# Down projection with tokens stationary: 128 tokens of g held, 512 columns of w_out moving

## The chip, the cores and the metric

The kernel runs on one core of one Trainium2 chip. The metric is the device time of one execution in microseconds (us). Before the change it is 959.91 us, the median of three runs (959.44 to 959.99).

Engines are named as in the profile: PE (TensorE matmul) with PEld (its weight loads), DVE (VectorE), ACT (ScalarE), POOL (GpSimd), and SP, whose queue issues all DMAs here.

## The reference

Attention over 8 batches, 8 heads, 576 positions and 64 dimensions, in two parts that are added: a pooled one (q, k and v averaged over groups of four positions, softmax over 144 pooled keys, the result repeated four times) and a local one (softmax over keys less than four positions away). The heads are joined to 512 features per token, and the 4608 tokens go through two projections.

```python
out_d = sm_attn(q_d, k_d, v_d)               # pooled by 4
out_up = np.repeat(out_d, factor, axis=2)
mask = np.abs(pos[:, None] - pos[None, :]) < factor
out_local = softmax(where(mask, scale * q @ k.T, -1e9)) @ v
x = (out_up + out_local).transpose(0, 2, 1, 3).reshape(B * S, H * D)
h = x @ w_in                                  # 512 -> 2048
g = np.maximum(0.01 * h, h)
return g @ w_out                              # 2048 -> 512
```

## The kernel before, in words

**Tokens in chunks.** `plan` (L42) cuts the tokens into 13 chunks, the columns of one matmul. Batch 0 makes chunk 0 (256 tokens) and chunk 1 (320). Batches 1 to 7 have 9 blocks of 64 tokens each (a block is every ninth position), and `SIZES` deals the 63 blocks out: 4, 5 and then 6 to a chunk, so 256, 320 and nine times 384 columns. A chunk is made of segments of at most `MAXSEG` blocks of one batch; PARTS lists them by batch.

**Three matmuls for each product.** Weights, x and g are kept as a high part that the fast float32 matmul takes exactly and a low part that is the rest. A product is high by high, high by low and low by high.

**Up projection** (`up_proj`, L689). For each chunk and each f of 16 slices of 128 features of h, twelve matmuls (four slices of x, three products) fill a bank `hp` with 128 features by the chunk's tokens. `leaky` (L712) then makes the high part gh and the activation itself by ACT (L716, L717), and the low part gl by DVE (L719).

**Down projection** (`down_proj`, L724). For each f and each e of four slices of 128 output features, three matmuls (L746) hold 128 by 128 of w_out in the array and move gh or gl, the chunk's tokens being the columns; they add into bank `acc{e}`. The result is the output transposed (features by tokens). After the last f, `store` (L765) copies each bank to a buffer `o` (two of them) and writes it out.

**Passes.** Weights for f = 8 to 15 come late (their memory is given back by batch 0's attention, `swap`, L792). So PASSES runs chunk 0 and chunk 1 over f = 0 to 7, then both over f = 8 to 15, and then each later chunk over all 16. The half sums are stored to the output in memory, loaded again (`refetch`, L757) and added by DVE (L771).

**Making x.** Batch 0 goes through PE with banded scores (`banded`, L434); its two halves fill x of chunks 0 and 1. For later batches the local part is done per segment and pair of heads: `scores` (L548) and `values` (L602) let POOL multiply into `prod` (L567, L628) and DVE add up (L573, L634); `landing` (L658) transposes the result by PE (L665), adds the pooled part (L672) and writes the high part by ACT (L678) and the low part by DVE (L680). The pooled part (`pooled`, L330) is scores by PE (L358), softmax by ACT and DVE, transposes (L397) and values (L409). x has two pairs of buffers, for even and odd chunks; a chunk's x may be written once the chunk two before it is done.

**Weights.** `convert` (L255) loads 512 KB of a float64 weight slice into a staging buffer, builds float32 from its bits by ACT (L268) and DVE (L270), makes the high part by ACT (w_in, L281) or DVE (w_out, L278), and the low part by POOL (L283). Staging buffers are borrowed from k, v, prod and up for f below 10 and from v, up and vs after, with two x buffers besides for the first four.

**Order.** Nothing is ordered on the chip but by waits. `Order` (L98) runs all of this as tasks in a model with costs for each engine (COST, RATE, HOP) and a buffer count for each tag (`bufs`, L190); at each step it emits the operation that the model could start first, at equal times the one with the smallest rank. Up and down projection have the last ranks (4999, 5000). So each engine's queue is a fixed list, and a wrong cost in the model shows as a wait. Small matmuls use two banks `pt`; batch 0 may use the accumulators and `hp` until the up projection has started (`banks`, L291).

Of the kernel before, what the change touches and what calls it, by code (L numbers as in the profile page):

```python
# [27 lines left out]
MAXSEG = 4  # L28
SIZES = (4, 5, 6, 6, 6, 6, 6, 6, 6, 6, 6)
QB = 48  # L30
FSPLIT = 8
OWN = 10
# [40 lines left out]
LANDED = [NC, NC] + [2 * sum(len(pieces(a, z)) for _, a, z, _ in c[2]) for c in CHUNKS[2:]]  # L73
XMAX = [max(c[1] for c in CHUNKS[i::2]) for i in range(2)]
OMAX = max(XMAX)
# [11 lines left out]
class Slot:  # L87
    def __init__(self, order, tag, index, t, task):
        self.order, self.tag, self.index, self.t, self.task = order, tag, index, t, task
        self.push = HURRY if tag in SCARCE else 0  # L90
        task[0] -= self.push
# [91 lines left out]
def attn_moe(ctx: ExitStack, tc, qkt, vd, qb, kb, vb, vwb, band, identb, w_in, w_out, ident, edge, out):  # L183
# [6 lines left out]
    bufs = dict(head=HEADS, qk=1, vs=1, qk_d=2, v_d=1, su_vd=2, su_half=1, su_pd=3, su_ptd=2, st_d=3, pd=2, ptd=1, outd=2, q=1, k=1, v=1, s=3, st_l=3, prod=2, up=1,  # L190
                xloc=2, lst=3, gh=3, gl=3, o=2, hp=2, pt=2, xh0=1, xl0=1, xh1=1, xl1=1, acc0=1, acc1=1, acc2=1, acc3=1,
# [3 lines left out]
    def slot(*tags):  # L195
        return (yield ("slot", tags, 0))
# [24 lines left out]
    def wait(name, n=1):  # L221
        return (yield ("wait", name, n))
# [32 lines left out]
    def convert(f, k):  # L255
        s = yield from slot(*(("k", "v", "prod", "up") if f < OWN else ("v", "up", "vs")), *(("xh1", "xl1") if f < 4 else ()))
# [25 lines left out]
        t = yield from op("POOL", 590, t)  # L282
        nc.gpsimd.tensor_tensor(out=lo, in0=tf, in1=hi.bitcast(F32), op=ALU.subtract)  # L283
# [4 lines left out]
    xt = {}  # L288
    kept = {}
# [11 lines left out]
    def x_tile(i):  # L301
        if i > 1:
# [27 lines left out]
    def pooled(b, c, rank, pool=None):  # L330
# [20 lines left out]
        s_st, s_pd = (yield from slot("st_d")), (yield from slot("su_pd" if pool else "pd"))  # L351
# [10 lines left out]
        st, pd = sb(s_st, [128, 2, 3], F32), sb(s_pd, [128, 3, SD], F32, pool)  # L362
# [71 lines left out]
    def banded(b, c, hf, rank, pool=None):  # L434
# [90 lines left out]
        t = yield from op("ACT", n, t, tx)  # L525
        nc.scalar.copy(out=xh[:, c], in_=av[:, :n])
        t = yield from op("DVE", n, t)
        nc.vector.tensor_tensor(out=xl[:, c], in0=av[:, :n], in1=xh[:, c].bitcast(F32), op=ALU.subtract)
        s_b.free(t)
        od.signal(("x", hf), t)  # L530
# [71 lines left out]
    def values(i, b, j0, j1, c0, u):  # L602
# [4 lines left out]
        s_v = yield from slot("v")  # L607
# [79 lines left out]
    reload = {}  # L687
# [36 lines left out]
    def down_proj():  # L724
        for i, (p, f) in enumerate(steps):
            ch, f0, f1 = PASSES[p]
            n = CHUNKS[ch][1]
            per = 0.012 + n / 2400
            if f == f0:
                accs[p] = {}  # L730
            if f == f0 + 2 and f0 > 0:
                for e in range(NE):
                    od.spawn(50, refetch(p, e, n))
            tg = yield from wait(("g", i))
            tw = yield from wait(("w", f, 1))
            s_g, s_l, gh, gl = gs.pop(i)
            wh, wl = (w.rearrange("p c m -> p (c m)") for w in weight(f, 1))
            for e in range(NE):
                if f == f0:
                    s_a = yield from slot(f"acc{e}")  # L740
                    accs[p][e] = s_a, bank(s_a)
                s_a, acc = accs[p][e]
                es = slice(e * 128, (e + 1) * 128)
                t = yield from op("PE", 3 * per, tg, tw, s_a.t)
                for j, (wt, g) in enumerate(((wh, gh), (wh, gl), (wl, gh))):
                    nc.tensor.matmul(acc[:, :n], wt[:, es], g[:, :n],  # L746
                                     start=f == f0 and j == 0, stop=f == f1 - 1 and j == 2)
# [5 lines left out]
    def dest(p, e, n):  # L753
        base = CHUNKS[PASSES[p][0]][0]
        return out[e * 128:(e + 1) * 128, base:base + n]

    def refetch(p, e, n):  # L757
        s_o = yield from slot("o")
        o = sb(s_o, [128, OMAX], F32)
        tw = yield from wait(("half", PASSES[p][0]), 4)  # L760
        t = yield from load(o[:, :n], dest(p, e, n), 512 * n, s_o.t, tw)
        reload[p, e] = s_o, o
        od.signal(("reload", p, e), t)

    def store(p, e, n, s_a, acc, t):  # L765
        key, f0, f1 = PASSES[p]
        if f0 > 0:
            tr = yield from wait(("reload", p, e))
            s_o, o = reload.pop((p, e))
            t = yield from op("DVE", n, t, tr)  # L770
            nc.vector.tensor_tensor(out=o[:, :n], in0=acc[:, :n], in1=o[:, :n], op=ALU.add)  # L771
        else:
            s_o = yield from slot("o")
            o = sb(s_o, [128, OMAX], F32)
            if p == len(PASSES) - 1 and e % 2:
                t = yield from op("DVE", n, t, s_o.t)
                nc.vector.tensor_copy(out=o[:, :n], in_=acc[:, :n])
            else:
                t = yield from op("ACT", n, t, s_o.t)
                nc.scalar.copy(out=o[:, :n], in_=acc[:, :n])  # L780
        s_a.free(t)
        t = yield from load(dest(p, e, n), o[:, :n], 512 * n, t)
# [49 lines left out]
_OUTS = [((DM, B * S), 'float32')]  # L832
# [56 lines left out]
```

## Time and profile before

| | |
|---|---|
| time, median of three runs | 959.91 us |
| span of the profiled execution | 957.9 us |
| PE busy | 932.4 us, 97% |
| POOL busy | 617.8 us, 64% |
| DVE busy | 595.2 us, 62% |
| ACT busy | 415.0 us, 43% |
| mean granted clock of PE | 0.996 |

The span runs from the first to the last instruction of the program; the time of an execution is larger by what lies around it. A busy share is an average over the span. Matmuls are pipelined: a matmul's recorded length (some 0.34 us at 384 columns) overlaps those of its neighbours, so the price of one in a stream is the distance between starts. Line numbers (L746) are those of the kernel before. In the lists of waits a row reads: who waited, for whom, us in total, times, longest. In the groups: count, busy us, mean ns of one, idle time before them and what ended it.

### The profile page before, as it was taken

The numbers are of one execution on the slowest core, as the hardware profiler recorded it, in microseconds if no ns is written. First come the engines' busy times: TensorE is split into PE (matmuls) and PEld (weight loads), VectorE is DVE, ScalarE is ACT, GpSimd is POOL, SyncE is SP. The second block draws the span as 40 slices with busy tenths as digits, with TensorE's granted clock in tenths as the row PEclk, the third lists the DMA queues.
The fourth block names the chain that finished last, engine by engine and source line by source line (L and its number), as shares of the span: only waits on it lengthen the run. The fifth ranks groups of instructions, "written<-read, shape, count | busy, mean of one in ns | idle before, by whom it ended". The sixth has DMA issues, their size and how long they took to land.

```text
span 957.9 us, 16170 instructions
## 1 busy us (share of the span) xinstructions
PE 932.4 (97%) x6282; PEld 894.8 (93%) x6282; DVE 595.2 (62%) x895; ACT 415.0 (43%) x1139; POOL 617.8 (64%) x356
## 2 busy tenths in 40 slices
PE   6799999999999999999999999999999999999997
PEld 5588999899999999999999999899999999999997
DVE  5986678888887776787657774862753753311111
ACT  3774555555545543445324553532513423422211
POOL 3759868777888778986798776884885873100000
PEclk9899999999999999999999999999999999999999
DMA  9755665644554523452424442431231220000000
GB/s 264 241 184 181 214 201 179 189 164 145 188 166 122 190 96 116 131 187 95 135 74 146 159 148 101 140 116 58 92 116 58 91 77 31 34 1 1 34 1 33
DMA packets 63180, 117.31 MB, mean 122 GB/s; under 512 B 4944, under 2 KB 32848, under 8 KB 63104
## 3 DMA queue, kind: packets, MB, share of 16 engines
q1 hardware_dynamic: 63104, 116.29, 38.6%
q8 instruction: 49, 0.80, 0.4%
q14 instruction: 27, 0.22, 0.1%
HBM read 105.65 MB, written 10.62 MB: 121 GB/s over the span
## 4 chain that ended last, share of the span: by engine, by line
PE 77%; POOL 8%; DMA 4%; issue 4%; DVE 4%; ACT 2%; SPq 0%; POOLq 0%; DVEq 0%; ACTq 0%
PE hp L706 35%; PE acc L746 34%; POOL prod L567 4%; POOL prod L628 3%; PE pt L358 2%; DMA k<-in_kb_dram 2%; PE pt L397 2%; PE pt L409 2%; PE pt L665 1%; DMA qk<-in_qkt_dram 1%; DVE s L573 1%; DMA v<-in_w_in_dram 0%; SPq L218 0%; DMA vs<-in_w_out_dram 0%; DVE gl L719 0%
## 5 line engine op out<-in xcount | busy, mean ns | idle before, releaser
L567 POOL TENSOR_TENSOR prod<-q,k 128x1344 f32<-128x1344 f32 (+1 forms) x88 | 266.3, 3027 | 81.3 <-DMA k<-in_kb_dram 55.2
L628 POOL TENSOR_TENSOR prod<-v,s 128x1344 f32<-128x1344 f32 (+1 forms) x88 | 265.6, 3021 | 32.3 <-DVE xloc L634 18.2
L706 PE MATMUL hp<-xh,wih 128*128 128x384 f32 (+2 forms) x832 | 279.9, 336 | 5.8 <-DVE gl L719 5.1
L746 PE MATMUL acc<-gh,woh 128*128 128x384 f32 (+2 forms) x832 | 274.4, 330 | 0.3 <-ACT o L780 0.3
L706 PE MATMUL hp<-xl,wih 128*128 128x384 f32 (+2 forms) x832 | 269.5, 324 | 0.3 <-DVE xl L680 0.3
L706 PE MATMUL hp<-xh,wil 128*128 128x384 f32 (+2 forms) x832 | 269.6, 324 | 0.0
L746 PE MATMUL acc<-gh,wol 128*128 128x384 f32 (+2 forms) x832 | 269.0, 323 | 0.0
L746 PE MATMUL acc<-gl,woh 128*128 128x384 f32 (+2 forms) x832 | 268.9, 323 | 0.0
L719 DVE TENSOR_TENSOR gl<-hp,gh 128x384 fp32r<-128x384 f32 (+2 forms) x208 | 108.5, 522 | 215.7 <-ACT hp L717 215.2
L716 ACT ACTIVATE gh<-hp 128x384 fp32r<-128x384 f32 (+2 forms) x208 | 97.3, 468 | 315.6 <-PE acc L746 307.9
L706 PEld LDWEIGHTS hp<-xh,wih 128*128 128x128 f32 x832 | 156.4, 188 | 15.6 <-DVE gl L719 8.0
L746 PEld LDWEIGHTS acc<-gh,woh 128*128 128x128 f32 x832 | 156.2, 188 | 4.0 <-issue 3.2
L706 PEld LDWEIGHTS hp<-xl,wih 128*128 128x128 f32 x832 | 156.7, 188 | 0.5 <-DVE xl L680 0.5
L706 PEld LDWEIGHTS hp<-xh,wil 128*128 128x128 f32 x832 | 156.4, 188 | 0.0
L746 PEld LDWEIGHTS acc<-gl,woh 128*128 128x128 f32 x832 | 156.3, 188 | 0.0
L746 PEld LDWEIGHTS acc<-gh,wol 128*128 128x128 f32 x832 | 156.2, 188 | 0.0
L573 DVE TENSOR_REDUCE s<-prod 128x21 f32<-128x1344 f32 (+1 forms) x88 | 130.2, 1479 | 27.9 <-POOL prod L567 27.9
L634 DVE TENSOR_REDUCE xloc<-prod 128x192 f32<-128x1344 f32 (+1 forms) x88 | 130.1, 1478 | 22.5 <-POOL prod L628 22.1
L717 ACT ACTIVATE hp<-hp 128x384 f32<-128x384 f32 (+2 forms) x208 | 96.1, 462 | 0.0
L672 DVE TENSOR_TENSOR pt<-pt,up 128x384 f32<-128x384 f32 (+1 forms) x44 | 37.8, 861 | 27.6 <-PE pt L665 22.2
L652 ACT COPY up<-outd 128x576 f32<-128x576 f32 x84 | 52.3, 675 | 0.0
L370 ACT ACTIVATE pd<-pt,st_d 128x144 f32<-128x144 f32 x84 | 32.1, 382 | 46.4 <-DVE st_d L367 35.4
(154 smaller groups left out, 754.3 us busy)
## 6 DMA issues: line engine op xcount, KB each, us to landing
k<-in_kb_dram SPq DMA_DIRECT2D x38, 576.0 KB
v<-in_vb_dram SPq DMA_DIRECT2D x38, 576.0 KB
qk<-in_qkt_dram SPq DMA_DIRECT2D x32, 576.0 KB
vs<-in_vd_dram SPq DMA_DIRECT2D x28, 288.0 KB
q<-in_qb_dram SPq DMA_DIRECT2D x38, 192.0 KB
out_dram<-o SPq DMA_DIRECT2D x36, 192.0 KB
v<-in_w_out_dram SPq DMA_DIRECT2D x4, 512.0 KB
prod<-in_w_out_dram SPq DMA_DIRECT2D x4, 512.0 KB
```

The source lines that it names most:

```text
L370: nc.scalar.activation(out=pd[:, qi], in_=scv[:, qi], func=AF.Exp, scale=SCALE / (FAC * FAC), bias=mx[:, qi:qi + 1], accum_out=sm[:, qi:qi ...
L567: nc.gpsimd.tensor_tensor(out=prv, in0=q[:, p, a - j0:z - j0].unsqueeze(2).to_broadcast([128, n, W, D]), in1=view(k[:, p], (a - j0) * D, [ ...
L573: nc.vector.tensor_reduce(out=s[:, p, a - j0:z - j0], in_=prv, axis=AX.X, op=ALU.add)
L628: nc.gpsimd.tensor_tensor(out=prv, in0=view(v[:, p], a - j0, [[1, n], [nv, D], [1, W]]), in1=s[:, p, a - j0:z - j0].unsqueeze(2).to_broadc ...
L634: nc.vector.tensor_reduce(out=xl_t[:, :n, p], in_=prv, axis=AX.X, op=ALU.add)
L652: nc.scalar.copy(out=up[:, pp], in_=outd[b][:, 2 * u + pp].unsqueeze(2).to_broadcast([128, SD, FAC]))
L672: nc.vector.tensor_tensor(out=xv, in0=xv, in1=upv, op=ALU.add)
L706: nc.tensor.matmul(hp[:, :n], wt[:, c], x[:, c], start=k == 0, stop=k == 3 * NC - 1)
L716: nc.scalar.activation(out=gh[:, :n], in_=hp[:, :n], func=AF.Prelu, alpha=0.01)
L717: nc.scalar.activation(out=hp[:, :n], in_=hp[:, :n], func=AF.Prelu, alpha=0.01)
L719: nc.vector.tensor_tensor(out=gl[:, :n], in0=hp[:, :n], in1=gh[:, :n].bitcast(F32), op=ALU.subtract)
L746: nc.tensor.matmul(acc[:, :n], wt[:, es], g[:, :n], start=f == f0 and j == 0, stop=f == f1 - 1 and j == 2)
```

## The change

- **Down projection.** Now 128 tokens of gh or gl are held in the array and all 512 columns of a slice of w_out move. A chunk has two or three tiles of 128 tokens, each with a bank `acc{m}`, and the output is written as tokens by features.
- **First chunks kept in PSUM.** Chunk 0 uses banks 0 and 1, chunk 1 banks 2 and 3, and they stay until f = 15; storing, loading and adding half sums go. Once chunk 1 is stored, bank 3 is given to the small matmuls as a third bank besides the two `pt`.
- **Chunks.** All are multiples of 128 tokens: 256, 256, 256 and ten times 384. Batch 0's last 64 tokens ride at the end of chunk 2 (`TAIL`), behind three blocks of batch 1. Segments have at most three blocks.
- **Stores.** A tile leaves in two halves of 256 columns, each with its own copy and DMA (`send`), from three buffers `o`; in the last chunk DVE takes every second copy.
- **Buffers.** A new tag `w2` serves as a second v buffer and as staging for weights. su_pd goes from 3 to 2, pd from 2 to 1, s and st_l from 3 to 2.
- **Low parts.** For f from 8 on (`LOV`) the low part of a weight is made by DVE.

```diff
-MAXSEG = 4
-SIZES = (4, 5, 6, 6, 6, 6, 6, 6, 6, 6, 6)
+MAXSEG = 3
+SIZES = (3,) + (6,) * 10
+TT = 128
+OW = 256
-OWN = 10
+OWN, LOV = 10, 8
+STAGE = "w2", "up", "v"
-    chunks, at = [(0, 256, ()), (256, 320, ())], S
+    chunks, at = [(0, 256, ()), (256, 256, ())], 512
+        n += i == 0
+TAIL = (2, CHUNKS[2][1] - 64)
+X0 = 256 - TAIL[1]
...
     def convert(f, k):
-        s = yield from slot(*(("k", "v", "prod", "up") if f < OWN else ("v", "up", "vs")), *(("xh1", "xl1") if f < 4 else ()))
+        s = yield from slot(*(("k", "v", "w2", "prod", "up") if f < OWN else STAGE), *(("xh1", "xl1") if f < 4 else ()))
...
-        t = yield from op("POOL", 590, t)
-        nc.gpsimd.tensor_tensor(out=lo, in0=tf, in1=hi.bitcast(F32), op=ALU.subtract)
+        if f >= LOV:
+            t = yield from op("DVE", 512, t)
+            nc.vector.tensor_tensor(out=lo, in0=tf, in1=hi.bitcast(F32), op=ALU.subtract)
+        else:
+            t = yield from op("POOL", 590, t)
+            nc.gpsimd.tensor_tensor(out=lo, in0=tf, in1=hi.bitcast(F32), op=ALU.subtract)
...
     def banks(b):
+        if "spare" in od.events:
+            return "pt", "acc3"
...
     def values(i, b, j0, j1, c0, u):
-        s_v = yield from slot("v")
+        s_v = yield from slot("v", "w2")
...
     def down_proj():
+        per = 0.0133 + DM / 2400
         for i, (p, f) in enumerate(steps):
             ch, f0, f1 = PASSES[p]
-            n = CHUNKS[ch][1]
-            per = 0.012 + n / 2400
-            if f == f0:
-                accs[p] = {}
-            if f == f0 + 2 and f0 > 0:
-                for e in range(NE):
-                    od.spawn(50, refetch(p, e, n))
+            tiles = CHUNKS[ch][1] // TT
+            if f == 0:
+                accs[ch] = {}
...
-            for e in range(NE):
-                if f == f0:
-                    s_a = yield from slot(f"acc{e}")
-                    accs[p][e] = s_a, bank(s_a)
-                s_a, acc = accs[p][e]
-                es = slice(e * 128, (e + 1) * 128)
+            for m in range(tiles):
+                if f == 0:
+                    s_a = yield from slot(f"acc{m + 2 * (ch == 1)}")
+                    accs[ch][m] = s_a, bank(s_a)
+                s_a, acc = accs[ch][m]
+                ms = slice(m * TT, (m + 1) * TT)
                 t = yield from op("PE", 3 * per, tg, tw, s_a.t)
-                for j, (wt, g) in enumerate(((wh, gh), (wh, gl), (wl, gh))):
-                    nc.tensor.matmul(acc[:, :n], wt[:, es], g[:, :n],
-                                     start=f == f0 and j == 0, stop=f == f1 - 1 and j == 2)
-                if f == f1 - 1:
-                    od.spawn(-5, store(p, e, n, s_a, acc, t))
+                for j, (g, wt) in enumerate(((gh, wh), (gh, wl), (gl, wh))):
+                    nc.tensor.matmul(acc, g[:, ms], wt, start=f == 0 and j == 0, stop=f == NF - 1 and j == 2)
+                if f == NF - 1:
+                    od.spawn(-5, store(ch, m, s_a, acc, t))
...
+    def store(ch, m, s_a, acc, t0):
+        rows = CHUNKS[ch][0] + m * TT
+        ends = []
+        for h in range(DM // OW):
+            cols = slice(h * OW, (h + 1) * OW)
             s_o = yield from slot("o")
+            o = sb(s_o, [128, OW], F32)
+            if ch == len(CHUNKS) - 1 and h % 2:
+                t = yield from op("DVE", OW, t0, s_o.t)
+                nc.vector.tensor_copy(out=o, in_=acc[:, cols])
             else:
+                t = yield from op("ACT", OW, t0, s_o.t)
+                nc.scalar.copy(out=o, in_=acc[:, cols])
+            ends.append(t)
+            if h == DM // OW - 1:
+                s_a.free(max(ends))
+                if ch == 1 and m == 1:
+                    od.signal("spare", max(ends))
+            od.spawn(-4, send(out[rows:rows + TT, cols], o, s_o, t))
```

More of the change, by code (lines that the diff above doesn't have):

```diff
@@ L70, in pieces @@
     return list(zip(cuts, cuts[1:]))
-LANDED = [NC, NC] + [2 * sum(len(pieces(a, z)) for _, a, z, _ in c[2]) for c in CHUNKS[2:]]
-XMAX = [max(c[1] for c in CHUNKS[i::2]) for i in range(2)]
-OMAX = max(XMAX)
+TAIL = (2, CHUNKS[2][1] - 64)
+X0 = 256 - TAIL[1]
+LANDED = [NC, NC] + [(NC if c is CHUNKS[2] else 0) + 2 * sum(len(pieces(a, z)) for _, a, z, _ in c[2]) for c in CHUNKS[2:]]
+OMAX = max(c[1] for c in CHUNKS)
+assert all(c[1] % TT == 0 for c in CHUNKS)
 COST = {"ACT": (0.13, 0.00083), "DVE": (0.08, 0.00104), "POOL": (0.25, 0.00217)}
@@ L89, in __init__ @@
         self.order, self.tag, self.index, self.t, self.task = order, tag, index, t, task
[L90 removed]
+        self.push = HURRY if tag in SCARCE or (tag == "acc3" and "spare" in order.events) else 0
         task[0] -= self.push
@@ L301, in x_tile @@
     def x_tile(i):
-        if i > 1:
+        if i == 2:
+            t = yield from wait(("done", 0), 2)
+            xt[i] = [x[:, :, X0:X0 + CHUNKS[i][1]] for x in whole]
+            od.signal(("xbuf", i), t)
+            return
+        if i > 2:
             yield from wait(("xbuf", i - 1))
@@ L306, in x_tile @@
         s_h, s_l = (yield from slot(f"xh{i % 2}")), (yield from slot(f"xl{i % 2}"))
-        xt[i] = [sb(t, [128, NC, XMAX[i % 2]], F32R)[:, :, :CHUNKS[i][1]] for t in (s_h, s_l)]
+        full = [sb(t, [128, NC, OMAX], F32R) for t in (s_h, s_l)]
+        if i == 0:
+            whole.extend(full)
+        xt[i] = [x[:, :, :CHUNKS[i][1]] for x in full]
         od.signal(("xbuf", i), max(s_h.t, s_l.t))
-        t = yield from wait(("done", i), 2 if i < 2 else 1)
+        t = yield from (wait(("done", 2 if i == 0 else i), 2 if i == 1 else 1))
         s_h.free(t)
@@ L524, in banded @@
         od.signal(("held", b))
[L525 to L528, printed above, removed]
+        places = [(hf, xh[:, c], xl[:, c], 0, CHUNKS[hf][1])]
+        if hf:
+            places.append((TAIL[0], *(x[:, c, X0 + TAIL[1]:X0 + TAIL[1] + 64] for x in whole), CHUNKS[1][1], 64))
+        for ch, hi, lo, o, m in places:
+            th = yield from op("ACT", m, t, tx)
+            nc.scalar.copy(out=hi, in_=av[:, o:o + m])
+            tl = yield from op("DVE", m, th)
+            nc.vector.tensor_tensor(out=lo, in0=av[:, o:o + m], in1=hi.bitcast(F32), op=ALU.subtract)
+            od.signal(("x", ch), tl)
+        t = tl
         s_b.free(t)
-        od.signal(("x", hf), t)
         if b == 0:
@@ L660, in landing @@
         tu = yield from wait(("up", b, j0, u))
-        s_b = yield from slot("pt")
+        s_b = yield from slot(*banks(b))
         xps = bank(s_b)
@@ L750, in down_proj @@
             s_g.free(t)
             s_l.free(t)
[L753 to L772, printed above, removed]
+    def store(ch, m, s_a, acc, t0):
[3 more added lines that the diff above has]
+            cols = slice(h * OW, (h + 1) * OW)
@@ L773, in store @@
             s_o = yield from slot("o")
[L774 to L777, printed above, removed]
-            else:
[L779 to L782, printed above, removed]
+            o = sb(s_o, [128, OW], F32)
@@ L783, in store, with send @@
+    def send(dst, o, s_o, t):
+        t = yield from load(dst, o, 128 * 4 * OW, t)
         s_o.free(t)
-        if f1 < NF:
-            od.signal(("half", key), t)
     su = tc.tile_pool(name="su", bufs=1)
```

27 lines of the change are left out of this document (17 added, 10 removed).

## The prediction, on record before the result

> **What bounds the kernel now.** The page comes first: which engine has no time left, and where in the span.
>
> ```profile
> span 957.9 us, 16170 instructions
> PE 932.4 (97%) x6282; PEld 894.8 (93%) x6282; DVE 595.2 (62%) x895; ACT 415.0 (43%) x1139; POOL 617.8 (64%) x356
> PE   6799999999999999999999999999999999999997
> PEclk9899999999999999999999999999999999999999
> ```
>
> PE is busy in every slice but the first two and the last, at the full granted clock after the first two; weight loads run beside the matmuls. The span is 957.9 us and the median of the three runs is 959.91, so 2.0 us lie outside the span. I sum against the span and add 2.0 at the end.
>
> A busy PE could still be waiting in small pieces, so the second view is the stretches (start, first projection steps, second stretch to chunk 2, chunk 2, chunk 3, the rest) and the third the waits of PE's own queue.
>
> ```profile
> core 0: us, PE busy (x) PEld busy (x) DVE busy (x) ACT busy (x) POOL busy (x), PEclk, DMA share, GB/s
> 0.00:44.00 44.00, 30.24 (x338) 22.67 (x340) 31.59 (x65) 25.24 (x76) 23.73 (x26) 0.92 0.92 272
> 44.00:72.00 28.00, 25.73 (x270) 24.30 (x265) 24.71 (x45) 20.42 (x48) 16.73 (x13) 1.00 0.53 162
> 72.00:169.00 97.00, 95.01 (x729) 90.44 (x728) 72.64 (x114) 52.07 (x146) 78.62 (x51) 1.00 0.61 191
> 169.00:226.00 57.00, 55.34 (x482) 52.20 (x481) 48.03 (x83) 32.24 (x104) 41.66 (x26) 1.00 0.56 183
> 226.00:292.00 66.00, 66.00 (x501) 62.37 (x500) 54.40 (x82) 36.39 (x114) 56.92 (x31) 1.00 0.48 151
> 292.00:958.00 666.00, 660.10 (x3978) 642.81 (x3977) 363.88 (x509) 248.65 (x654) 400.16 (x213) 1.00 0.29 93
> ```
>
> ```profile
> PE hp L706 <- DVE gl L719: 5.1, 10, 1.4
> PE hp L706 <- ACT xh L678: 0.7, 1, 0.7
> PE hp L706 <- DVE xl L680: 0.3, 1, 0.3
> ```
>
> From 44 us on PE has about 11 us without work (2.3, 2.0, 1.7, 0 and 5.9 by stretch, most of the last after the final matmul). So time is a sum of PE work; only two things can move it: fewer or cheaper matmuls, and a supply of x that comes too late for PE.
>
> **Down projection.** I need the start-to-start price of a matmul by columns. The chain of waits merges runs of matmuls that follow without a gap: start, length, count.
>
> ```profile
> 207.62 2.75 PE acc L746 x24
> 94.82 3.52 PE acc L746 x24
> 944.64 7.29 PE acc L746 x42
> 196.00 1.43 PE hp L706 x12
> 72.29 3.52 PE hp L706 x24
> 934.07 4.22 PE hp L706 x24
> ```
>
> By the start times these are 256 columns (2.75/24 = 114.6 ns), 320 (3.52/24 = 146.7) and 384 (7.29/42 = 173.6) in the down projection, and 119, 146.7 and 175.8 ns in the up projection. The counts by shape, one of three equal groups each:
>
> ```profile
> L746 PE MATMUL acc<-gh,woh 128*128 128x384 f32 x576 | 197.0, 342 | 0.0
> L746 PE MATMUL acc<-gh,woh 128*128 128x320 f32 x128 | 40.8, 319 | 0.3 <-ACT o L780 0.3
> L746 PE MATMUL acc<-gh,woh 128*128 128x256 f32 x128 | 36.5, 286 | 0.0
> ```
>
> Before: 1728 x 173.6 + 384 x 146.7 + 384 x 114.6 ns = 300.0 + 56.3 + 44.0 = 400.3 us. After: 36 blocks of 128 tokens x 16 x 3 = 1728 matmuls of 512 columns. No row has 512. The last 64 columns that the rows show cost 26.9 ns (146.7 to 173.6), so 128 more would cost 53.8: 227.4 ns, and 1728 of them 393.0 us. That saves **7.3 us**: 768 matmuls fewer, each with a price that its columns don't explain. The ends: the two rows of 384 columns differ by 2.2 ns, so some 2 less, 225.4 ns at the best (389.5, saves 10.8), and the 320 row scaled to 512, 234.7 ns, at the worst (405.6, loses 5.3). I take 227.4 because the step from 320 to 384 lies nearest to 512.
>
> The Trainium skill (TensorE: Matmul & The Clock Gate, "Wait — 56ns, not 53.3ns?") gives N / 2.4 + about 2.5 ns for matmuls back to back, which is 162.5 for 384 columns where the row has 173.6; by it 768 matmuls fewer are worth only 1.9 us, and the sum would say 5 us less gain. The measured excess of 11 ns decides for me, though it doesn't say whether it goes with the matmul or with the columns; that is a rival below.
>
> **Up projection.** Chunk 1 gets 256 columns for 320 and chunk 3 gets 384 for 320; the 64 tokens left of batch 0 make chunk 2 up to 256 with three blocks. Of 2496 matmuls 384 + 384 + 1728 become 576 + 1920: 45.7 + 56.3 + 303.8 = 405.8 us before, 68.5 + 337.5 = 406.0 after. 0.2 us lost. Transposes and scores of PE stay the same, and so do the elements that POOL multiplies.
>
> **First chunks kept in PSUM.** Eight loads of half sums, eight stores and eight additions go; the additions are VectorE's.
>
> ```profile
> L771 DVE TENSOR_TENSOR o<-acc,o 128x320 f32<-128x320 f32 x4 | 1.9, 484 | 0.0
> L771 DVE TENSOR_TENSOR o<-acc,o 128x256 f32<-128x256 f32 x4 | 1.5, 414 | 0.6 <-DMA o<-out_dram 0.6
> ```
>
> That is 3.4 us of VectorE, off PE's path: nothing on PE. The four banks stay occupied over both passes, as PE never waited for them but 0.3 us (the row of L746 above); once chunk 1 is stored the fourth serves transposes. By the code SP issues 72 stores where it issued 60 and 8 loads: nothing.
>
> **Late low parts to VectorE.** The rows of POOL's low parts and of VectorE's own two-operand step on the same staging tile, each in 71 to 125 us:
>
> ```profile
> 71.00:125.00 54.00, 21.85 (x16) 1.00 0.63 196
> 71.00:125.00 54.00, 12.37 (x11) 1.00 0.63 196
> L719 DVE TENSOR_TENSOR gl<-hp,gh 128x384 fp32r<-128x384 f32 x144 | 79.8, 555 | 204.1 <-ACT hp L717 203.7
> ```
>
> The first (L283) says that POOL loses 16 x 1.37 = 21.9 us. VectorE gains between 16 x 0.555 (a subtraction of 384 elements with one operand in PSUM) = 8.9 and 16 x 1.12 (the second, L270) = 18.0; I take 16 us, because L270 like the new step has both operands in SBUF while POOL works. Less 3.4 of additions: VectorE +13, POOL -22, until chunk 3. The Trainium skill (SBUF — State Buffer, "SBUF: two separate sides") says that a VectorE step with two SBUF inputs and a GpSimd step exclude each other for a whole instruction, which speaks against the move: POOL would be held while VectorE subtracts. The long mean of L270, twice that of L719, agrees.
>
> **Is x there in time?** What the supply has to meet is when PE took each chunk up, and the last low part of its x:
>
> ```profile
> 169.06 0.36 PE L706 MATMUL hp<-xh,wih 128*128 128x256 f32 x1
> 170.63 0.74 DVE L680 TENSOR_TENSOR xl<-pt,xh 128x256 fp32r<-128x256 f32 x2
> 224.91 0.41 DVE L680 TENSOR_TENSOR xl<-pt,xh 128x256 fp32r<-128x256 f32 x1
> 225.71 0.31 PE L706 MATMUL hp<-xh,wih 128*128 128x320 f32 x1
> 290.45 0.54 DVE L680 TENSOR_TENSOR xl<-pt,xh 128x384 fp32r<-128x384 f32 x1
> 292.41 0.34 PE L706 MATMUL hp<-xh,wih 128*128 128x384 f32 x1
> ```
>
> Chunk 2's x came late (PE stood 0.7 + 0.3 us), chunk 3's 0.4 us ahead, chunk 4's 1.4 us ahead. The change asks for it sooner. Ahead of chunk 2 PE loses 192 x (146.7 - 119) = 5.3 us of up and 6.4 of chunk 1's down (28.2 to 96 x 227.4 = 21.8), 0.2 of chunk 0's: it is there at 157.2. Chunk 3, again 0.2 less of down, at 213.6, but still with nine blocks due. Chunk 4 gets 5.6 + 4.5 us back: 290.5. So nine blocks are due 12.1 us earlier. From 72 us to there POOL has 78.6 + 41.7 - 21.9 = 98.4 us of work in 141.6 (69%) and VectorE 72.6 + 48.0 + 13 = 133.6 (94%). Some 9 us of that VectorE work was ahead for chunk 4 (three score tasks at two reductions of 1.48 us, the row below), which the two score buffers now hold back, so 88%; the stretch 44 to 72 ran at 24.71 of 28, 88%. It fits, barely. The weights of f = 8 to 15 are due sooner too, by half of the 11.9 us that PE loses there; their conversion comes out of the same 133.6 us. I take back the 1.0 us of chunk 2's wait as a gain and put 1 us for new waits of PE on VectorE (bounds 0 and 12.1, the last worked out with the rivals). The second v buffer takes waits from POOL only.
>
> ```profile
> L573 DVE TENSOR_REDUCE s<-prod 128x21 f32<-128x1344 f32 (+1 forms) x88 | 130.2, 1479 | 27.9 <-POOL prod L567 27.9
> ```
>
> **Stores and the end.** A chunk now leaves in six copies of 256 columns through three buffers, before four of 384 through two.
>
> ```profile
> L780 ACT COPY o<-acc 128x256 f32<-128x256 f32 x8 | 2.8, 375 | 0.9 <-DMA out_dram<-o 0.9
> 952.54 1.86 DMA out_dram<-o
> 953.91 0.48 ACT L780 COPY o<-acc 128x384 f32<-128x384 f32 x1 [2.00 <-DMA out_dram<-o]
> 954.53 0.56 DVE L777 COPY o<-acc 128x384 f32<-128x384 f32 x1 [2.01 <-DMA out_dram<-o]
> ```
>
> At the end the last pair of copies waited 2.0 us for a buffer, and still will, as copies 4 to 6 need the buffers of 1 to 3; a copy is 0.15 us shorter, a tile comes every 0.68 us instead of 0.52. I put 0, bounds -0.5 and +0.5. Within the run the copies wait likewise. Counted from the first finished tile, copies by ACT at 0.375 and a buffer back after 1.86, the second tile's bank is free at 2.65 us and the next chunk's down projection, if it followed at once, wants it at 2.04: 0.6 us, and 0.1 for the third. One step of up projection (2.1 us) between covers it, and the chain shows runs of up and down in turn. Nothing, at most 12 x 0.7 = 8.4 us.
>
> **Sum.** -7.3 + 0.2 - 1.0 + 1.0 = -7.1: span 950.8, time **952.8 us**.
>
> **The rivals.**
> - *Supply decides (slower).* If VectorE's load eats what POOL gives up, nine blocks are still ready at 225.3 and chunk 3 starts at 225.7 instead of 213.6. PE idles 12.1 us; all the work moved behind that point (+10.3 for chunk 3, -5.2 for nine chunks of 192 x 173.6 becoming 144 x 227.4) remains: 959.9 + 5.1 = 965. It eats the whole gain once chunk 3 starts after 213.6 + 7.1 = 220.7. For it: 94% of VectorE, one score and one pd buffer fewer. Against: POOL's 22 us, shorter VectorE steps beside an idler POOL, one block fewer ahead of chunk 2. Chance 0.10.
> - *The price goes with the columns (no change).* From 256 to 384 a column costs (173.6 - 114.6)/128 = 0.461 ns, which gives 232.6 ns at 512 and 401.9 us: 1.6 lost, 961.7 with 0.2 more for up and the waits as above. The Trainium skill's 2.5 ns per matmul would put the rest of the excess there too. For it: 256 columns pay little excess. Against: 320 to 384, the rows nearest. With half of it, 958. Chance 0.13.
> - *Early waits vanish as well (faster still).* Of PE's 5.1 us for gl only 0.8 lie behind 226 us (the row below, of that stretch alone); the rest falls where VectorE and ACT convert weights. A further staging buffer and no additions could end most, and 225.4 ns saves 10.8: 959.9 - 10.8 - 1.0 - 4 = 944. Chance 0.15.
>
> ```profile
> PE hp L706 <- DVE gl L719: 0.8, 2, 0.6
> ```
>
> The forecast has 0.62, with 947 to 957 as its own range; it reaches over it by DVE waits and by the price of a matmul. The whole range is **944 to 962**: it takes in the columns rival and half of the supply one. A measurement of this kernel can tell about 0.2%, 1.9 us: faster is below 958.0. The forecast, the third rival and a little of the second make 0.80 faster; the second gives most of 0.11 same; the first and a little of the second 0.09 slower.
>
> **What would show it.** Right: clean runs of L746 at 227 to 228 ns a matmul, 1728 of them; the same early PE waits within 2 us; chunk 3 (the first of 384 columns) taken up near 214 us. Wrong: 232 ns or more; PE waiting for xh or xl before chunk 3; PE waiting at L746 for the copies of the accumulators.

## The result and the profile after

The changed kernel takes 974.43 us (median of seven runs, 964.65 to 976.86) against 959.99 of the kernel before: ratio 1.0123, 95% interval 1.0093 to 1.0152. It is slower by 1.2% by this ratio (14.4 us between the medians); 952.8 was forecast. Its runs lie far apart, and with them the granted clock of TensorE: 0.990 in the run of 964.65, 0.971 in the profiled one of 975.98 (span 974.2).

From the page after:

```profile
span 974.2 us, 14646 instructions
PE 941.7 (97%) x5514; PEld 823.3 (85%) x5514; DVE 601.7 (62%) x896; ACT 416.8 (43%) x1160; POOL 587.7 (60%) x332
PE   5898899999999999999999999999999999999997
POOL 3662216798888888996687784587577696200000
PEclk9588899999999999999999999999999999999999
```

PE is as full as before and executes 768 matmuls fewer, yet is busy 9 us longer. Three things are new: the clock is low up to the fifth slice, PE has holes in the second, fourth and fifth, and POOL does next to nothing from the fourth to the sixth. The waits of PE's own queue:

```profile
PE hp L731 <- DVE gl L744: 8.0, 3, 3.9
PE acc L768 <- ACT o L786: 2.5, 1, 2.5
```

Before it was 5.1 us in ten waits of at most 1.4; now it is 8.0 in three. (In this kernel the up projection is L731, the down projection L768, gl L744, the copies of the accumulators L786 and L783, the products L593 and L654, the low part by VectorE L290, the cast of w_out L284.)

Where the time went, from the starts of the matmuls in the two traces (us):

| | first up step | chunk 3 taken up | chunk 5 taken up | from there to the last down matmul |
|---|---|---|---|---|
| before | 44.2 | 225.7 | 372.6 | 580.0 |
| after | 46.2 | 236.3 | 384.0 | 584.4 |

Up to chunk 5 both kernels have done the same 1536 tokens. Of the 16.3 us of span 11.4 are lost ahead of it, 4.4 behind it, and 0.4 behind the last matmul. Chunk 3 compares less well: the plans put different numbers of PE's small matmuls (transposes, pooled scores and values) ahead of it, 677 before and 729 after, and 927 of both ahead of chunk 5.

**Ahead of chunk 5.** The second stretch of projection steps, before and after:

```profile
72.00:130.00 58.00, 56.01 (x421) 53.98 (x420) 38.93 (x57) 30.30 (x75) 45.84 (x31) 1.00 0.66 207
```
```profile
72.00:130.00 58.00, 51.01 (x327) 43.57 (x327) 47.75 (x65) 29.32 (x82) 14.55 (x8) 0.85 0.49 160
```

The third to fifth figures with counts are DVE, ACT and POOL. DVE took on 9 us. POOL gave up 31, more than the 22 of its low parts: its products moved back, not forward. (Experiment 3 shows that this alone costs little.) The timeline around PE's longest wait shows the mechanism (start, length):

```profile
82.78 6.50 POOL L593 TENSOR_TENSOR prod<-q,k 128x1344 f32<-128x1344 f32 x2 [10.09 <-DVE wol L290]
83.80 2.60 DVE L284 CAST woh<-up 128x512 fp32r<-128x512 f32 x1
85.91 0.39 PE L768 MATMUL acc<-woh,gl 128*128 128x512 f32 x1
86.32 3.51 DVE L290 TENSOR_TENSOR wil<-v,wih 128x512 fp32r<-128x512 f32 x1
89.75 0.41 DVE L744 TENSOR_TENSOR gl<-hp,gh 128x256 fp32r<-128x256 f32 x1
90.22 0.58 PE L731 MATMUL hp<-xh,wih 128*128 128x256 f32 x1 [3.92 <-DVE gl L744]
```

POOL waited 10.1 us for VectorE's low part, because staging tile and product buffer are the same memory. Then its two products of 3.2 us ran from 82.8 to 89.3; VectorE's cast of w_out (L284) began at 83.8 beside the first and ended 0.3 us behind it, and its subtraction (L290) began at 86.3 beside the second and ended 0.55 us behind it, five times its usual 0.68. gl stood behind both, and PE behind gl. The same again near 112 us, where a cast takes the part of the subtraction:

```profile
111.29 3.50 POOL L593 TENSOR_TENSOR prod<-q,k 128x1344 f32<-128x1344 f32 x1
111.81 3.27 DVE L284 CAST woh<-v 128x512 fp32r<-128x512 f32 x1
116.59 0.58 PE L731 MATMUL hp<-xh,wih 128*128 128x256 f32 x1 [3.06 <-DVE gl L744]
```

After each of the two waits the clock is halved for a while; PEclk is the third figure from the right:

```profile
88.30:95.10 6.80, 4.88 (x18) 4.40 (x19) 6.58 (x11) 2.09 (x6) 0.98 (x1) 0.50 0.61 193
115.60:125.80 10.20, 9.21 (x41) 8.31 (x42) 8.82 (x14) 3.21 (x7) 0.53 (x2) 0.50 0.68 217
```

So a wait of 3 to 4 us is paid again afterwards, with up to 3.4 and 5.1 us of work at half speed. The kernel before has no wait over 1.4 us from its first projection step on, and no halved stretch between that step and its last matmul.

The halved clock is most of what is new. From the first up step to chunk 3 PE is idle 8.1 us after and 5.9 before (stretches of 190.1 and 181.5 us, PE busy 182.06 and 175.59). But the clock is halved for 25.0 us of it after and for none before: 17.1 behind the two waits and 8.0 left from the start, where it was halved from 23.4 to 54.1 us (before: 35.1 to 42.0, over by the first step). What sets the clock of the start no run tells. Behind 130 us nothing more is lost ahead of chunk 3; PE is busy, at the full clock:

```profile
130.00:236.00 106.00, 105.55 (x742) 91.17 (x740) 82.97 (x135) 59.43 (x193) 75.55 (x41) 1.00 0.51 162
```

**Behind chunk 5.** The chain of waits in the last chunk, before and after; each row is two steps (two f) of down projection:

```profile
896.38 4.16 PE acc L746 x24
904.73 4.16 PE acc L746 x24
```
```profile
904.28 4.13 PE acc L768 x18
920.95 4.19 PE acc L768 x18
929.34 4.20 PE acc L768 x18
```

Two steps of 384 tokens took 4.16 us in 24 matmuls and take 4.13 to 4.20 in 18. A matmul of 512 columns costs 229 to 233 ns; by these rows the turned projection gains nothing. The 4.4 us lost are mostly one wait for the copies of an accumulator, with 3.4 us of halved clock behind it:

```profile
708.11 0.37 ACT L786 COPY o<-acc 128x256 f32<-128x256 f32 x1 [3.67 <-DMA out_dram<-o]
708.53 0.50 PE L768 MATMUL acc<-woh,gh 128*128 128x512 f32 x1 [2.48 <-ACT o L786]
```

The copy waited 3.7 us for its buffer to be sent; PE, which had the next chunk's tile for that bank, waited for the copy.

### The profile page after: what moved, and what is told of

Same layout as the page of the kernel before. It is cut to its first block, busy times and chain, and to the rows that moved or that the text cites. A ratio compares the mean times of both kernels' runs of the same rounds, so it can differ in the third digit from the quotient of the medians.

```text
span 974.2 us, 14646 instructions
## 1 busy us (share of the span) xinstructions
PE 941.7 (97%) x5514; PEld 823.3 (85%) x5514; DVE 601.7 (62%) x896; ACT 416.8 (43%) x1160; POOL 587.7 (60%) x332
## 4 chain that ended last, share of the span: by engine, by line
PE 86%; DVE 4%; DMA 4%; POOL 3%; issue 1%; ACT 1%; SPq 0%; DVEq 0%; ACTq 0%; POOLq 0%
PE hp L731 39%; PE acc L768 38%; PE pt L430 2%; PE pt L379 2%; POOL prod L654 1%; PE pt L418 1%; DMA k<-in_w_in_dram 1%; POOL prod L593 1%; DMA su_vs<-in_vd_dram 1%; PE pt L691 1%; DMA out_dram<-o 1%; PE acc L379 1%; DVE woh L284 1%; DVE wil L290 1%; PE acc L418 1%
## 5 line engine op out<-in xcount | busy, mean ns | idle before, releaser
L593 POOL TENSOR_TENSOR prod<-q,k 128x1344 f32<-128x1344 f32 x84 | 260.4, 3105 | 52.8 <-DMA k<-in_kb_dram 37.0
L731 PE MATMUL hp<-xh,wih 128*128 128x384 f32 (+1 forms) x832 | 282.0, 339 | 8.6 <-DVE gl L744 8.0
L731 PE MATMUL hp<-xh,wil 128*128 128x384 f32 (+1 forms) x832 | 272.2, 327 | 0.0
L731 PE MATMUL hp<-xl,wih 128*128 128x384 f32 (+1 forms) x832 | 271.9, 327 | 0.0
L744 DVE TENSOR_TENSOR gl<-hp,gh 128x384 fp32r<-128x384 f32 (+1 forms) x208 | 108.6, 523 | 213.2 <-ACT hp L742 211.5
L768 PE MATMUL acc<-woh,gh 128*128 128x512 f32 x576 | 233.1, 405 | 2.5 <-ACT o L786 2.5
L768 PE MATMUL acc<-wol,gh 128*128 128x512 f32 x576 | 227.8, 396 | 0.0
L768 PE MATMUL acc<-woh,gl 128*128 128x512 f32 x576 | 227.6, 395 | 0.0
L731 PEld LDWEIGHTS hp<-xh,wih 128*128 128x128 f32 x832 | 159.5, 192 | 23.7 <-DVE gl L744 11.5
L731 PEld LDWEIGHTS hp<-xl,wih 128*128 128x128 f32 x832 | 159.8, 192 | 3.8
L731 PEld LDWEIGHTS hp<-xh,wil 128*128 128x128 f32 x832 | 159.5, 192 | 0.0
L654 POOL TENSOR_TENSOR prod<-v,s 128x1344 f32<-128x1344 f32 x42 | 130.9, 3119 | 34.5 <-DVE xloc L660 32.6
L660 DVE TENSOR_REDUCE xloc<-prod 128x192 f32<-128x1344 f32 x84 | 129.8, 1546 | 25.7 <-POOL prod L654 25.6
L654 POOL TENSOR_TENSOR prod<-w,s 128x1344 f32<-128x1344 f32 x42 | 130.6, 3117 | 4.1 <-issue 2.4
L768 PEld LDWEIGHTS acc<-woh,gl 128*128 128x128 f32 x576 | 108.9, 189 | 25.5
L768 PEld LDWEIGHTS acc<-woh,gh 128*128 128x128 f32 x576 | 109.1, 189 | 23.8 <-issue 3.2
L768 PEld LDWEIGHTS acc<-wol,gh 128*128 128x128 f32 x576 | 109.0, 189 | 17.5
L606 POOL TENSOR_TENSOR s<-s,edge_sb 128x42 f32<-128x42 f32 x42 | 11.4, 270 | 58.4 <-DVE s L599 52.9
```

The source lines that it names most:

```text
L593: nc.gpsimd.tensor_tensor(out=prv, in0=q[:, p, a - j0:z - j0].unsqueeze(2).to_broadcast([128, n, W, D]), in1=view(k[:, p], (a - j0) * D, [ ...
L654: nc.gpsimd.tensor_tensor(out=prv, in0=view(v[:, p], a - j0, [[1, n], [nv, D], [1, W]]), in1=s[:, p, a - j0:z - j0].unsqueeze(2).to_broadc ...
L660: nc.vector.tensor_reduce(out=xl_t[:, :n, p], in_=prv, axis=AX.X, op=ALU.add)
L731: nc.tensor.matmul(hp[:, :n], wt[:, c], x[:, c], start=k == 0, stop=k == 3 * NC - 1)
L744: nc.vector.tensor_tensor(out=gl[:, :n], in0=hp[:, :n], in1=gh[:, :n].bitcast(F32), op=ALU.subtract)
L768: nc.tensor.matmul(acc, g[:, ms], wt, start=f == 0 and j == 0, stop=f == NF - 1 and j == 2)
```

## Theories and experiments

Theory A: VectorE's steps on staging tiles stand behind GpSimd's products, gl behind them, PE behind gl. Theory B: a matmul's price goes with its columns. Theory E: a wait costs a halved clock behind it. Against A: the other edits (buffers, chunks dealt anew) or VectorE's mere load. The table at the end has the stages of all kernels.

**1. Low parts back on GpSimd.**

```diff
-OWN, LOV = 10, 8
+OWN, LOV = 10, 16
```

> The changed kernel, but with all low parts of the weights made by GpSimd again (LOV = 16). Theory A (VectorE's low parts stand behind GpSimd's products, PE waits for gl behind them and its clock is halved afterwards): L290's steps of 3.3 to 3.5 us go, PE's waits for gl fall from 8.0 to under 5 us, the granted clock comes back from 0.971 to 0.985 or more, time 956 to 963. Rival C (the early loss comes from the other edits: fewer score and pd buffers, chunks due earlier, staging): time stays at 970 or above with chunk 3 taken up at 230 us or later.

967.60 us, ratio 1.0077 (1.0052 to 1.0101), clock 0.981 in the profiled run: between the ranges of A and C. Some 7 of the 14 us between the medians go, 4.4 of 11.8 us by the ratios. The long waits for gl at 86 and 113 us are gone, though PE still waits 6.6 us for gl in all, 3.1 of them at 48. Chunk 3 is taken up at 228.3. So A holds for a third to a half of the loss in this run, which also gives GpSimd its 22 us back; experiment 3 parts the two.

**2. The kernel before with low parts of late weights on VectorE alone.**

```diff
-        t = yield from op("POOL", 590, t)
-        nc.gpsimd.tensor_tensor(out=lo, in0=tf, in1=hi.bitcast(F32), op=ALU.subtract)
+        if f >= 8:
+            t = yield from op("DVE", 512, t)
+            nc.vector.tensor_tensor(out=lo, in0=tf, in1=hi.bitcast(F32), op=ALU.subtract)
+        else: ...
```

> The kernel before with only one edit: low parts for f from 8 on by VectorE. Theory A: 966 to 975, with VectorE low parts of over 3 us and PE waiting for gl more than the 5.1 us of before. Rival C: 958 to 962, the low parts at 0.7 to 1.1 us each.

969.32 us, ratio 1.0097 (1.0082 to 1.0113): this one edit makes the old kernel slower by some 9 us. Its steps reach 2.6 us (L284 of this kernel, min/median/max):

```profile
L284 DVE TENSOR_TENSOR wil<-v,wih x3: 685/907/2615, 74.5 to 109.9; 128x512 fp32r<-128x512 f32 x3
L284 DVE TENSOR_TENSOR wol<-up,woh x2: 693/1664/2636, 80.5 to 102.5; 128x512 fp32r<-128x512 f32 x2
```

Chunk 3 is taken up at 235.5, 9.8 us later than before: the start is 1.4 later, PE is idle 8.8 us from there to chunk 3 (before 5.9), and the clock is halved for 11.2 us of it (before none), which costs at most 5.6. Of the idle time 4.4 us are for gl (before 4.2) and 4.2 for xl of chunk 2 (before 1.0 for xh and xl). So part of the loss is late x at chunk 2, and a larger part the halved clock. PE's longest wait for gl (1.8 us) stands behind another held step of VectorE, the bit step (1.61 us for 0.69), not behind a low part. That the edit costs 9 us is shown; on which way, only in part.

**3. The same place and size, but one operand.** This tells the shared reading from the load. The subtraction is left out: the low part holds the whole value.

```diff
-            nc.vector.tensor_tensor(out=lo, in0=tf, in1=hi.bitcast(F32), op=ALU.subtract)
+            nc.vector.tensor_reduce(out=lo, in_=tf.unsqueeze(2), axis=AX.X, op=ALU.add)
```

> The changed kernel, with VectorE's subtraction for the low part (two operands in SBUF) replaced by a sum over an axis of one element (one operand, the same 512 elements, same place in every queue). The subtraction is left out: the low part holds the whole value. Theory A in its narrow form (the subtraction stands because it shares a read port with GpSimd's products): its steps take 0.6 to 0.8 us each, none over 1 us; the waits of PE for gl fall from 8.0 to some 4 us (the casts of w_out may still stand), time 966 to 971. Rival (the work itself on VectorE is too much): steps of over 3 us don't matter or stay, time 973 or more.

962.99 us, ratio 1.0024 (1.0006 to 1.0042): 9.5 us less than the changed kernel by the ratios, below what either theory expected, with the same list of operations in every queue. The largest groups of the step, changed kernel and this one:

```profile
L290 DVE TENSOR_TENSOR wil<-v,wih 128x512 fp32r<-128x512 f32 x3 | 4.9, 1631 | 0.1
L290 DVE TENSOR_TENSOR wil<-w,wih 128x512 fp32r<-128x512 f32 x3 | 4.7, 1567 | 0.2 <-ACT wih L287 0.2
```
```profile
L291 DVE TENSOR_REDUCE wil<-v 128x512 fp32r<-128x512 f32 x3 | 2.0, 672 | 0.0
L291 DVE TENSOR_REDUCE wil<-w 128x512 fp32r<-128x512 f32 x3 | 2.0, 670 | 0.0
```

All at 0.67 us, none held. The step that took 3.51 us beside GpSimd's second product stands in the same place here, beside the same product:

```profile
81.15 6.32 POOL L594 TENSOR_TENSOR prod<-q,k 128x1344 f32<-128x1344 f32 x2 [10.01 <-DVE wol L291]
82.16 2.36 DVE L284 CAST woh<-up 128x512 fp32r<-128x512 f32 x1
84.44 0.67 DVE L291 TENSOR_REDUCE wil<-v 128x512 fp32r<-128x512 f32 x1
```

The cast ahead of it is still held. And from 72 to 130 us, where the changed kernel had PE at 51.01 and the clock at 0.85:

```profile
72.00:130.00 58.00, 57.18 (x412) 48.79 (x410) 51.01 (x87) 36.87 (x103) 14.03 (x10) 1.00 0.60 192
```

VectorE does more than in the changed kernel (51.01 for 47.75) and POOL as little (14.03 for 14.55), after the same wait of 10 us for a low part. Chunk 3 is taken up at 222.4, chunk 5 at 371.9 (before: 372.6). From the first up step to chunk 3 PE is idle 1.7 us for 8.1 and the clock is halved for 6.6 us for 25.0; 6.4 us of waits and at most 9.2 of work at half speed are enough for the 13.0 us by which that stretch is shorter. So what VectorE was given is not too much in amount, and POOL's standing is not the loss; the second operand in SBUF is what held the step. (The sum doesn't read the high part either, so it needn't wait for the cast; the subtractions stood 0.2 us for that in all.) Against experiment 1 (1.0077) the move off GpSimd is then worth some 5 us. The Trainium skill (SBUF — State Buffer, "SBUF: two separate sides") says that a VectorE step with two SBUF inputs and a GpSimd step exclude each other for a whole instruction, and that a step in VectorE's two-port mode does too; the subtraction, the cast (3.27 us beside a product, 0.42 alone) and this run agree.

**4. The old down projection in the changed kernel, low parts on GpSimd.** w_out stationary, `acc{e}`, half sums stored and loaded again, as in `down_proj`, `store` and `refetch` before.

```diff
-            for m in range(tiles):
+            for e in range(NE):
...
-                    nc.tensor.matmul(acc, g[:, ms], wt, start=f == 0 and j == 0, stop=f == NF - 1 and j == 2)
+                    nc.tensor.matmul(acc[:, :n], wt[:, es], g[:, :n],
+                                     start=f == f0 and j == 0, stop=f == f1 - 1 and j == 2)
```

> As the run with all low parts on GpSimd, but with the down projection of before: w_out stationary, the chunk's tokens moving, half sums of chunks 0 and 1 stored and loaded again. Theory B (a matmul's price goes with its columns, so the turned down projection gains nothing): within 3 us of the run with low parts on GpSimd, rows of 384 columns at 173 to 176 ns. Rival D (the turned projection does gain its 7 us and the early stage hides it): 6 to 9 us slower than that run.

964.86 us, ratio 1.0060 (1.0041 to 1.0078), against 1.0077 (1.0052 to 1.0101) with the turned one: no gain by turning. The difference of 1.6 us is smaller than either interval reaches to a side, so no loss by turning is shown either. From chunk 5 to the last down matmul it takes 581.3 us for 582.9. B holds; D, which expected it to be 6 to 9 us slower, falls.

**5. Matmuls of 256 columns in the turned projection**, but for the first and the last of each tile.

```diff
-                    nc.tensor.matmul(acc, g[:, ms], wt, start=f == 0 and j == 0, stop=f == NF - 1 and j == 2)
+                    ...
+                    for h in range(2):
+                        hs = slice(h * OW, (h + 1) * OW)
+                        nc.tensor.matmul(acc[:, hs], g[:, ms], wt[:, hs], start=False, stop=False, skip_group_check=True)
```

> The changed kernel with the down matmuls cut into two of 256 columns in the same bank (46 of the 48 for each tile; the first and the last stay whole), so nearly twice as many matmuls and weight loads for the same columns. Theory B (price by columns): a pair costs 229 to 236 ns, like one of 512 (229 to 233). Fixed price per matmul (some 14 ns above the columns at 2.4 per ns): a pair costs 241 ns, and a step of nine tiles' products takes 2.17 us for 2.08.

One run: 973.31 us. Two steps are now 36 matmuls for 18 of 512:

```profile
850.60 4.20 PE acc L773 x36
875.74 4.24 PE acc L773 x36
```

4.20 to 4.24 us for 4.13 to 4.20: 18 matmuls more cost some 0.05 us, about 3 ns each. The forecast's step of 26.9 ns for 64 columns leaves 12.2 ns of 173.6 to the matmul itself, and 18 of these would be 0.22 us. B holds: 0.45 ns a column and some 3 ns a matmul. The Trainium skill's 2.5 ns per matmul, measured on bf16 (TensorE: Matmul & The Clock Gate, "Wait — 56ns, not 53.3ns?"), agrees with this; its 2.4 columns per ns does not, for these rows of float32 give 2.2.

**6. Matmuls of no use in one wait.** In the run of experiment 1 PE stood 3.5 us ahead of chunk 3's last landing, and the clock was halved behind it.

```diff
+        if (i, landed[i]) == (3, 4):
+            wo = weight(0, 1)[0].rearrange("p c m -> p (c m)")
+            for _ in range(14):
+                nc.tensor.matmul(xps, wo[:, :128], wo, start=True, stop=True)
```

> The run with all low parts on GpSimd, plus 14 matmuls of 512 columns of no use ahead of the transposes of chunk 3's last landing, where PE waited 3.5 us and its clock was halved for 10.2 us after. The plan doesn't know of them, so every queue is else the same. Theory E (a wait of over about 2 us costs a halved clock after it, as much again as the wait): the halved stretch behind 223 us goes, chunk 5 is taken up 3 to 5 us earlier than in that run (378.4), time 2 to 5 us less. Rival F (the halved clock has no part in the loss; PE's work there is hidden by the late x): chunk 5 within 1 us or later by the fillers' 3 us.

967.80 us, ratio 1.0072 (1.0046 to 1.0098). The stretch in experiment 1 and here:

```profile
223.50:233.70 10.20, 9.47 (x39) 7.30 (x41) 7.59 (x11) 4.88 (x15) 9.25 (x6) 0.50 0.82 243
```
```profile
223.50:233.70 10.20, 8.55 (x48) 6.04 (x48) 8.15 (x14) 6.22 (x20) 10.12 (x6) 1.00 0.65 201
```

The halved clock is gone, so it comes of the wait. But chunk 5 is taken up at 378.7 us for 378.4, within the 1 us that rival F gave. From chunk 2's take-up it is 2.0 us faster (213.4 for 215.4), and the first up step was 2.2 later. E is right on the cause and too high on the price here: in experiment 1 the x of chunk 3 was complete at 228.3, just when PE took it up, so up to there a slow PE lost little.

**7. The kernel before with the buffers of the change**: second v buffer that also stages weights, one pd, two score buffers, `MAXSEG` 3 (the main lines).

```diff
-                su_pd=3, ... pd=2, ... v=1, s=3, st_l=3,
+                su_pd=2, ... pd=1, ... v=1, w2=1, s=2, st_l=2,
-        s_v = yield from slot("v")
+        s_v = yield from slot("v", "w2")
```

> The kernel before with only the buffers of the change: second v buffer that also stages weights, one pd and two score buffers, at most three blocks in a segment. Theory G (the 5 us that remain with the old down projection and low parts on GpSimd come from the buffers): 962 to 966. Rival H (they come from dealing the chunks anew, with x due sooner): 957 to 961.

963.36 us, ratio 1.0028 (1.0006 to 1.0049): some 3 us of loss, about half of what experiment 4 leaves (1.0060). The interval is as wide as the difference to either theory. What has the rest, no run tells; dealing the chunks anew is what is left of the change.

**8. Matmuls of no use in the kernel before's start**, five ahead of each transpose group of batch 0's first half.

> The kernel before with five matmuls of 512 bf16 columns of no use ahead of each transpose group of batch 0's first half, 40 in all, where PE waits. Theory E: the halved clock ahead of the first projection (35 to 42 us in the profile of before) goes and the first up step comes up to 2 us earlier, 957 to 959. If the fillers stand in the way of the attention, the first up step is later and the time 960 to 966.

962.68 us, ratio 1.0018 (1.0000 to 1.0036). The clock stays full from 19 us on, but the first up step comes at 48.3 us for 44.2, the second of the two outcomes expected. As an improvement it fails.

**9. Casts of w_out on ScalarE**, in the kernel before and in the changed kernel with low parts on GpSimd.

```diff
-        if k:
-            t = yield from op("DVE", 512, t)
-            nc.vector.tensor_copy(out=hi, in_=tf)
-        else:
-            t = yield from op("ACT", 512, t)
-            nc.scalar.copy(out=hi, in_=tf)
+        t = yield from op("ACT", 512, t)
+        nc.scalar.copy(out=hi, in_=tf)
```

> The kernel before with the high parts of w_out made by ScalarE as those of w_in are, so VectorE's casts, 0.4 to 2.3 us each, go. Theory A: VectorE is freed of 14 us of which most was standing behind GpSimd, PE's waits for gl fall under 5.1 us, time 955 to 960. Rival: ScalarE's own queue (gh) suffers instead, 960 to 964.

> The changed kernel with low parts on GpSimd and the casts of w_out on ScalarE: nothing of the weights' conversion on VectorE but the bit step. Theory A: 962 to 966, chunk 3 taken up earlier than the 228.3 us of the run with low parts on GpSimd. If the supply of x is bound otherwise, 967 or more.

The kernel before: 962.63 us, ratio 1.0017 (0.9998 to 1.0037), no gain; A had expected 955 to 960, so the held casts are not what this kernel loses time by. Its first up step comes 8.7 us earlier than before, and chunk 3 is taken up when it was:

```profile
35.53 0.39 PE L702 MATMUL hp<-xh,wih 128*128 128x256 f32 x1
225.49 0.41 PE L702 MATMUL hp<-xh,wih 128*128 128x320 f32 x1
```

225.5 us for 225.7. It is not the x of chunk 3 that holds PE there: its last low part is done at 218.6 us, where before it was 225.3. On the way PE is idle 9.8 us for 5.9, 3.4 us run at half clock, and 69 more small matmuls lie between the first up step and chunk 3; the earlier start was spent on these. The changed kernel: 959.96 us, ratio 0.9991 (0.9967 to 1.0014), 7.6 us less than with the casts on VectorE (967.60), below A's range and level with before.

**10. Four accumulator banks in turn**, in that last kernel: tiles of later chunks take whichever bank is free first, and none is lent out.

```diff
-        if "spare" in od.events:
-            return "pt", "acc3"
-                    s_a = yield from slot(f"acc{m + 2 * (ch == 1)}")
+                    s_a = yield from slot(*((f"acc{m + 2 * ch}",) if ch < 2 else ("acc0", "acc1", "acc2", "acc3")))
```

> The last run (low parts on GpSimd, casts on ScalarE) with the three tiles of later chunks taking whichever of the four accumulator banks is free first, and no bank lent to the small matmuls. In that run PE waited 2.7 us for the copies of one bank near 695 us and its clock was halved for 3.4 us after: some 4 us. If this wait is all that the accumulators cost, it goes and the time is 955 to 958, under both kernels. If the third bank for small matmuls was worth more, transposes wait and chunk 3 is taken up later than 226 us, 960 to 965.

**953.20 us, ratio 0.9942 (0.9921 to 0.9963): faster than both kernels.** PE no longer waits for a copy; gl is its largest wait but the first load of the band:

```profile
PE pt L475 <- DMA band_sb<-in_band_dram: 5.4, 1, 5.4
PE hp L725 <- DVE gl L738: 3.5, 4, 1.3
```

From chunk 5 on it takes 579.4 us for 583.3. By the ratios the step from experiment 9 is worth 4.7 us, so these 3.9 us may be most of it. The two profiled runs lie further apart (spans of 948.9 and 963.0 us, the fastest and the slowest of their kernels): the first up step is at 35.4 for 42.4 us, where the clock was full here from 15.6 us on and halved there from 23.1 to 43.6. Whether the banks have a part in that, no run tells.

The stages of all kernels, from the profiled runs (us). The small matmuls ahead of chunk 3 number 729 in the changed kernel and in experiments 3, 4 and 10, 740 in 1 and 5, 677 to 752 in the others, so chunk 5 is the better mark:

| experiment | first up step | chunk 3 | chunk 5 | from there to the last down matmul |
|---|---|---|---|---|
| 1 low parts on GpSimd | 43.4 | 228.3 | 378.4 | 582.9 |
| 2 before, low parts on VectorE | 45.6 | 235.5 | 381.4 | 580.9 |
| 3 one operand | 45.2 | 222.4 | 371.9 | 584.4 |
| 4 old down projection | 43.1 | 230.9 | 375.7 | 581.3 |
| 5 256 columns | 43.0 | 229.7 | 379.2 | 586.4 |
| 6 matmuls in the wait | 45.7 | 230.2 | 378.7 | 583.3 |
| 7 before, buffers | 43.1 | 234.8 | 374.6 | 580.7 |
| 8 before, matmuls at start | 48.3 | 229.6 | 376.5 | 580.4 |
| 9 before, casts on ScalarE | 35.5 | 225.5 | 372.4 | 581.2 |
| 9 changed, casts on ScalarE | 42.4 | 226.0 | 374.2 | 583.3 |
| 10 four banks in turn | 35.4 | 217.4 | 364.0 | 579.4 |

## Why the prediction was wrong, step by step

- **Price of a matmul of 512 columns: failed.** 227.4 ns was taken from the step between 320 and 384 columns and the rest called a price per matmul. The chain gives 229 to 233 ns (18 in 4.13 to 4.20 us), so 1728 cost 396 to 403 us where 400.3 were, about nothing gained in place of 7.3. The mis-sized choice was the last two rows alone: 26.9 ns for 64 columns was the smallest of the differences (the same step in the up projection's rows is 29.1), and 256 to 384 gave 232.6, the rival's value. Experiments 4 and 5 show that the price goes with the columns.
- **Late low parts on VectorE: the sum held, the step that took it as a load failed.** The price of 16 us came out (16.4 us for the 16 steps), but by luck: 14 of them took 0.67 to 0.69 us and two took 3.3 and 3.5. It was counted into a share of VectorE's time. What decided was single steps, these two and the casts beside them, held by a product ahead of gl (experiment 3). The prediction named that exclusion and spoke of POOL being held by VectorE; it was VectorE that was held, and PE behind it. "1 us for new waits" was 7.0 in two waits.
- **The clock was put at full: failed.** The prediction read it as 1.00 in every stretch but the first and had no term for a wait that lowers it. 25.0 us at half clock lie between the first up step and chunk 3, 17.1 of them behind those two waits; a wait's price is more than its length.
- **"Is x there in time": the forecast time failed, the worry did not come true.** Chunk 3 came at 236.3 us, neither the forecast 213.6 nor the supply rival's 225.7. But the rival's mechanism, PE idle for want of x, is not in the changed kernel: from 130 to 236 us PE was busy 105.55 of 106.00, and no wait for xh or xl ahead of chunk 3 stands in its list. PE came late by itself. POOL did 14.6 us of work in 72 to 130 where it had done 45.8, and experiment 3 has the same and takes chunk 3 up at 222.4. Experiment 1, with POOL loaded again, has x complete only when PE takes it up.
- **Stores: nothing was put, 8.4 us at most.** It was one wait of 2.5 us with 3.4 us of halved clock behind it, by a copy that waited 3.7 us for its buffer, not the 1.86 of the row used. Four banks in turn end it.
- **Right:** the up projection's price, the half sums (experiment 4 has them back and is not slower), and the end (0.4 us, within the bounds).

Of the loss of 1.23 points, by ratios: the second operand of the low parts has 1.0 (1.0123 to 1.0024), of which giving them back to GpSimd wins 0.5 (1.0077), and low parts on VectorE cost the old kernel 1.0 alone. The buffers cost the old kernel some 0.3. Four banks in turn win 0.5 in the last kernel, which bounds what the accumulators' wait has. What the new chunks have, no run tells. The parts overlap, as each plan orders all queues anew, and each has an uncertainty of some 0.2.

## What to carry to other kernels

Where a price per instruction is to be told from a price per element, take all rows of the trace and fit them, not the pair that lies nearest; if they allow both, the gain of larger instructions may be nothing. Work that is moved to another engine is not only load: look at the longest that one such step can take beside its old neighbour, and at what is queued right behind it. And look at the granted clock behind each wait of the engine that bounds the kernel: a hole of 3 us can cost more behind it than in it.

## What the runs showed of the hardware

- VectorE's subtraction of two SBUF operands took 0.68 us alone and 3.51 beside a product of GpSimd that it had to outwait; a cast 0.42 and 3.27. A sum over one operand stayed at 0.66 to 0.68, beside a product too.
- A wait of PE of some 2.4 us or more behind the first up step was followed by a halved clock of 3.4, 6.8 or 10.2 us in the changed kernel and in experiment 1. Shorter ones went both ways: 1.8 us was followed by 3.4 us of it in experiment 4 (at 122 us) and by none in experiment 7 (at 192 us). The Trainium skill (TensorE: Matmul & The Clock Gate, "The HAM clock gate (the "warmup" mystery)") has a window of 3.4 us that runs freely; these lengths, one to three times 3.4, agree.
- The same kernel ran in 964.65 to 976.86 us at granted clocks of 0.990 to 0.971. Where waits lie near the length at which the clock falls, a single run tells little.
- Matmuls of 256, 384 and 512 columns follow each other at 0.45 ns a column, 2.2 columns per ns, with the clock granted in full. Why not faster, no run tells.
